# Inverse of the 64x64 triangular blocks by 64x64 tile products, two units' products issued in turn, with a new order of all work

## Chip, cores and metric

The kernel runs on one core of one Trainium2 chip. The metric is the device time of one execution in microseconds; lower is better. All times in this document are microseconds unless ns stands beside them.

## What is computed

A delta-rule attention over 4 x 8 heads of 768 tokens with 48 channels, and behind it an MLP with tanh-GELU on the heads put side by side (3,072 tokens, 384 to 2,048 to 384). The reference, cut to its core:

```
k_n = k / (np.linalg.norm(k, axis=-1, keepdims=True) + 1e-06)
state = 0
for t in range(S):
    y[:, :, t] = np.einsum('bhd,bhde->bhe', q[:, :, t], state)
    v_old = np.einsum('bhde,bhd->bhe', state, kt)
    state = state + bt * np.einsum('bhd,bhe->bhde', kt, vt - v_old)
h = x @ w_in            # x: y of all heads side by side
g = 0.5 * h * (1.0 + np.tanh(c * (h + 0.044715 * h * h * h)))
out = g @ w_out
```

## The kernel before

The sequence is cut into 12 chunks of 64 tokens. A chunk `c` holds all 32 heads, in two units `u = 2c` and `2c + 1` of 16 heads, and a unit keeps its heads as 8 pairs: one head of a pair on partitions 0 to 63, the other on 64 to 127. Inside a chunk the recurrence becomes a triangular system of 64 x 64 per head, whose inverse is found by five steps of Newton's iteration, X <- X (2 - L X). So there are three kinds of work:

- `load`, `norms` and `prep(u)`: DMA of q, k and v, norms of k, casts, transposes (T on PE, or `turn` as a DMA), the Gram products (GM, GQ, G2, G), their masked eviction on DVE (`ln`, `wpm`, `wpq`, `wp`), and the inverse.
- `chain(c)`: the part that goes from chunk to chunk: K and Q (old state times k and q), R, U (inverse times right side), S (new state), O (output), X or `turnx` (transpose for the MLP).
- `mlp(c)`: 16 groups `up0` to `up15` of three matmuls 128x256, four GELUs on ACT, two times four `down` groups of four matmuls 128x384, copies Z, and the DMA of the result.

Each inverse step `i` of a unit is: product A (L575: 8 matmuls), `rt` on DVE (2 minus A, L587), product B (L575: 8 matmuls), eviction of B as the next iterate. The iterate is kept block-diagonal in `bd`, [128, 8, 128]: the two heads of a pair stand on the two diagonal 64 x 64 blocks, the other two blocks are zero. So one matmul with a full 128 x 128 array serves a pair of heads, and the eviction of B writes two halves: `bde` (two copies of 64 partitions), `bdf` (one such copy and one of 128 partitions that multiplies by 0 or 1), or `xi` and `bdc` (a dense copy, and then two copies from there). The first iterate is made from `ln` by `X10` and `X11`. U uses the same block-diagonal matrix.

Which engine does which operation, and in what order, is a table written out by hand, `ORDER`: one word for each operation, with its engine and its PSUM bank. `Flow.emit` goes through it, gives each operation the semaphore waits that its inputs and its PSUM bank need, and writes each engine's list in that order. An engine runs its list strictly in order. `fill` words are dummy matmuls 128x512 without a reader.

Each `e.matmul` becomes two PE instructions, a weight load and a matmul. PE's list of the kernel before has 5,490 matmuls and 106 instructions that only wait.

Of the kernel before, what the change touches and what calls it, by code (L numbers as in the profile page):

```python
# [12 lines left out]
C = 64  # L13
# [4 lines left out]
beta01:a one pad1 k0x1.11:a k0x0.01:a bdz0:g upone1 wz:d fill23@0 fill20@1 fill46@0 fill16@1 fill63@4 fill26@1 half:d fill25@0 fill12@2  # L18
fill54@5 ident pad3:g k0x0.10 tmplz:d tmpl0 k0x1.00:a k0x1.10:a k0x1.01:a mmup:d pad0 mmlo:d mlo0 fill64@0 k0x0.00 mlo1 tmpl1 two:d triln1:d
triwpm3:d triwpm1:d ladj16:d fill37@1 identf k0x0.11 ident2 ladj32:d fill28@4 sq.0a:d fill65@3 mup0 k1.00 fill56@4 sum.0a triln0:d fill41@1  # L20
fill52@6 beta00 betaT0@3 betaN000 betaN001 betaN010 betaN011 k1.01 epsb k1.10:a fill45@2 beta11:a k1.11 fill22@1 beta10 sq.0b:g tabS pow.0a
eps.0a twob:d J1.1@3 sum.0b q0.1 mup1 nsa.0a v0.11 inv.0a ib.0a upone0 v0.10 pow.0b fill55@2 q0.0:a eps.0b nsa.0b sq.1:d fill36@0 kb.0 kc.1
bdz1:g k2.10 fill49@2 inv.0b ib.0b:g kb.1:g betaT1@0 kc.0 Tc.1@1 fill9@2 betaA111 betaA110 betaA101 sum.1 pow.1 eps.1:g nsq.1:g kTc.1 q1.1
fill60@4 Tb.0@2 kTb.0 Tc.0@4 kTc.0 Tb.1@1 inv.1 triwpm0:d betaA100 ib.1 GM.0@6 ln.0 kb.3:g v1.11:a v0.01 X11.0 wpm.0 kTb.1:a GM.1@4 ln.1
X10.0 v0.00:a qb.0:a Tq.0@1 wpm.1 kc.3 Tk.3@2 triln3 A1.0@0 X10.1:d kTq.0 GQ.0@4 k2.00:a kTk.3:a q1.0:a X11.1 C1.1 rj1.1 rt1.0 B1.0@0 k2.01
pad2 kb.2 wpq.0 bde10.0 kc.2:d GM.3@6 ln.3 B1.1@1 bde10.1:d bde11.0 A2.0@0 rt2.0 bde11.1 A2.1@1 rt2.1 Tk.2@3 triwpm2 B2.0@2 B2.1@0 qb.1:a
v1.00 Tq.1@1 v1.10 v1.01 wpm.3 bde21.0:d k2.11 sq.2 sum.2 bde20.0 A3.0@2 fill1@4 fill4@5 fill42@4 fill14@5 q2.0 bdf20.1 bdf21.1:d A3.1@0
rt3.0 B3.0@2 kTk.2:a GM.2@4 rt3.1 triln2 ln.2 w2.1 qb.2:a bdz4:g bdz3:g X10.3 kTq.1:a X11.3 w1.1 A1.3@0 pad5:g pow.2 B3.1@1 k3.10 GQ.1@6
wpm.2 rt1.3 kc.5 k4.10 q2.1 bdf30.0 bdf31.0 A4.0@2 rt4.0 vs.1 B1.3@0 R0b.0:g bdf30.1 bdf31.1 A4.1@1 bdz2:g wpq.1 v2.00 bdf10.3 qb.3:g
eps.2:g B4.0@2 bde41.0 nsq.2:g bde40.0 X11.2 rt4.1 q3.0 X10.2 A1.2@4 rt1.2 B4.1@1 bde41.1:d w1.0 bde40.1 Tq.2@3 kTq.2 B1.2@4 bde10.2  # L30
triwpm4:g A5.0@5 rt5.0 A5.1@1 rt5.1 bde11.2 bdf11.3:d k3.01 B5.0@2 bde50.0 A2.2@3 rt2.2 B5.1@4 bde50.1:d bde51.0 k3.00 bde51.1 B2.2@0
bde21.2 bde20.2 inv.2 A2.3@1 rt2.3 R0a.0:g U.0@4 Un.0:d B2.3@1 A3.2@0 rt3.2 q4.0 Tq.3@2 O.0@4 On.0:d fill6@3 bde21.3 qb.5:g B3.2@0 bde20.3
A3.3@1 rt3.3 kTq.3:a GQ.3@6 X.0@2 xT.0:d B3.3@1 triwpm5:g bdf30.2 bdf31.2 A4.2@0 rt4.2 bdf30.3 bdf31.3:d up4.0@2 up12.0@4 up13.0 k3.11 wpq.3
ib.2:g kb.5:g B4.2@0 up5.0 up6.0 up7.0 up14.0 A4.3@1 up15.0 up0.0@6 q3.1 tabG bde41.2:d bde40.2 up1.0 up2.0 A5.2@0 rt4.3 gelu1.0 pad4:g
kb.4:g kc.7 up3.0 B4.3@1 w2.0 kc.4:g sq.3:g sum.3 k4.00 k5.10 q4.1 gelu3.0 gelu0.0 qb.4:g T.4@2 kT.4:a T.5@4 rt5.2 bde41.3:d bde40.3:d kT.5
pow.3 eps.3:g up8.0@6 up9.0 v2.11 A5.3@0 rt5.3 k5.00:a G2.5@2 ln.5 bdz5:g kc.6:g X11.5 k4.01:a G2.4@4 S.0@0 Sn.0 ln.4 X11.4 X10.4 G.4@2 wp.4
up10.0 qb.9:a up11.0 gelu2.0 nsq.3:g qb.6:g qb.7:g k4.11 K.1@0 R.1 inv.3 ib.3:g kb.6:g kb.7:g v3.11 G.5@4 wp.5 B5.2@2 sq.4 down10.0@3 A1.4@1
down00.0@0 bde51.2 rt1.4 kc.8 down01.0 X10.5 sum.4 pow.4 eps.4:g B5.3@4 bdf50.3 B1.4@1 bde10.4 k5.01 bde11.4:d down11.0 A1.5@5 rt1.5
down02.0 k5.11 sq.5:g kc.10:g A2.4@1 v4.10 v4.11 rt2.4 turn.7 v2.10 bdf51.3 bde50.2 B1.5@4 bde10.5:d bde11.5 down03.0 Z0.0 B2.4@2 v3.10
bde21.4:d kc.9:g U.1@6 Un.1 A2.5@5 rt2.5 q5.0 down12.0 GQ.2@0 wpq.2 Q.1@6 bde20.4 A3.4@2 turn.6 v3.00:a rt3.4 G2.7@4 O.1 On.1 S.1@0 Sn.1  # L40
nsq.4:g down13.0 inv.4 ib.4:g X.1@2 B2.5@6 xT.1:d kb.9:g v4.01 sum.5 pow.5 eps.5:g kb.8:g Z1.0 bde20.5 B3.4@7 bdf30.4 turn.9 fill47@3 v3.01
ln.7 bdf31.4 v2.01:a up0.1@0 up1.1 up2.1 up3.1 bde21.5:d gelu0.1 q6.1 A4.4@2 rt4.4 qb.8:a up8.1@4 up9.1 k7.00 A3.5@3 rt3.5 B4.4@2 bde41.4
k7.11 G2.6@0 ln.6 G.7@6 wp.7 q7.0 up10.1 B3.5@3 bde31.5 bde30.5 X10.6 up11.1 gelu2.1 up4.1@0 up5.1 up6.1 G.6@6 bde40.4:d A4.5@3 k6.10:a
up7.1 down10.1@2 wp.6 k7.10 rt4.5 A5.4@4 rt5.4 up12.1@6 out11.0 gelu1.1 X11.6 A1.6@5 X11.7 X10.7 A1.7@3 rt1.7 rt1.6 k7.01 turn.8 B4.5@4
bdf40.5 q6.0 up13.1 B5.4@0 up14.1 xi5.4:d bdf41.5 B1.7@3 bdf10.7 bdc50.4 up15.1 B1.6@1 bdc51.4 bde10.6:d bde11.6 out00.0 vs.2 A5.5@5
down11.1 down12.1 q7.1 rt5.5 bdf11.7:d B5.5@5 nsa.5 gelu3.1 xi5.5 bdc50.5 A2.6@4 rt2.6 sq.7 Q.2@0 K.2@6 R.2 bdc51.5 A2.7@3 rt2.7 k6.00:a
B2.6@4 xi2.6:d bdc21.6 down00.1@5 U.2@6 Un.2 down01.1 B2.7@3 inv.5 sum.7 bde20.7:d fill27@4 O.2 bdc20.6 q5.1 G2.8@6 ln.8 A3.6@4 X10.8 ib.5:g
bde21.7 A3.7@3 rt3.7 On.2 X11.8 turnx.2 v4.00:a down13.1 Z1.1 rt3.6 G.8@6 wp.8 k6.01 vs.3 k6.11 B3.7@0 bde31.7 bde30.7 S.2@2 Sn.2 kb.10:g
B3.6@4 kb.11:g down02.1 bde30.6 A1.8@6 rt1.8 down03.1 bde31.6 kc.11:g qb.11:g Z0.1 out00.1 out11.1 A4.7@0 rt4.7 A4.6@2 B1.8@3 bdf10.8
bdf11.8 G.9@4 G2.9@6 ln.9 up4.2@0 up5.2 up6.2 B4.7@3 up7.2 up0.2@6 up1.2 up2.2 k8.10:a wp.9 rt4.6 up8.2@4 B4.6@2 bde41.6:d X11.9 bdf40.7  # L50
bdf41.7 gelu1.2 up9.2 up10.2 up11.2 up3.2 A2.8@3 qb.12:a up12.2@0 bde40.6:d A5.6@2 qb.10:g rt5.6 gelu2.2 gelu0.2 up13.2 A5.7@4 rt5.7 up14.2
rt2.8 B5.6@2 xi5.6 X10.9 A1.9@5 rt1.9 pow.7 sq.6:g B5.7@4 xi5.7 turn.10 sum.6 bdc50.7 up15.2 gelu3.2 down00.2@3 B2.8@2 bde21.8 bde20.8:d
k8.01 B1.9@4 bde10.9 K.3@6 R.3 G2.10@0 down10.2@5 q8.1 q8.0 turn.11 A3.8@2 rt3.8 kc.13:g eps.7:g bdc50.6 bdc51.6 down01.2 bdc51.7 U.3@6
# [12 lines left out]
bde50.10 up10.4 up11.4 turn.14 rt5.11 B5.11@2 up0.4@4 up1.4 up2.4 gelu2.4 nsq.8:g inv.8 bde51.10:d A2.13@0 up3.4 gelu0.4 xi5.11:d bdc51.11
# [730 lines left out]
```

## Time and profile before

| | us |
|---|---|
| median of 3 runs (262.59 to 270.14) | 262.89 |
| span of the profiled execution, first to last instruction | 258.8 |
| PE busy (matmuls, with their pipeline) | 242.1 |
| DVE busy | 209.5 |
| ACT busy | 185.1 |
| POOL busy | 136.2 |

The profile is one execution. Its rows give the engine, the line of the kernel, what is written from what, how many instructions of that kind, the busy time and the mean of one in ns; behind them stands the idle time just before these instructions and what ended it. "issue" means that the engine waited for nothing that the profile can name. The mean of a matmul holds its way through the array, some 190 ns for a narrow one; how fast matmuls follow each other is read from the timeline, where equal instructions that follow each other are one row with their start, length and count. In the windows view each row is a stretch: its length, PE's busy time with the number of matmuls, the granted clock, the busy share of the 16 DMA engines (it can pass 1 where packets run over the end of a window) and GB/s.

### The profile page before, as it was taken

How to read it: one execution, taken by the hardware profiler on the slowest of the kernel's cores; microseconds unless marked ns; L12 is line 12 of the kernel's file. 1: busy time of each engine (PE TensorE's matmuls, PEld its weight loads, DVE VectorE, ACT ScalarE, POOL GpSimd, SP SyncE). 2: the span in 40 equal slices, each digit the busy share in tenths (PEclk: the TensorE clock that was granted, in tenths of full speed). 3: DMA queues.
4: the chain of work that ended last, by engine and by line, in shares of the span. 5: the costliest groups of instructions: out<-in, count | busy, mean ns of one | idle time of the engine just before them, and what ended most of it. 6: DMA issues, size and time to landing. Idle time of an engine off the chain costs nothing.

```text
span 258.8 us, 12244 instructions
## 1 busy us (share of the span) xinstructions
PE 242.1 (94%) x5490; PEld 189.6 (73%) x5490; DVE 209.5 (81%) x358; ACT 185.1 (72%) x295; POOL 136.2 (53%) x198
## 2 busy tenths in 40 slices
PE   7769789998999999999999999989989999999994
PEld 2446669666867878778877787768868878877672
DVE  6898998988999798899999788997778879895000
ACT  0679899667786878687978879866948745754452
POOL 4469767997558978688158255643654204130000
PEclk9985999999999999999999999999999999999999
DMA  5999999879999877959729959536935720004122
GB/s 88 200 191 182 212 185 200 135 132 151 164 198 146 167 107 134 159 102 165 160 47 157 155 96 185 53 74 123 155 66 106 128 48 4 3 5 124 30 63 61
DMA packets 116788, 31.46 MB, mean 122 GB/s; under 512 B 110848, under 2 KB 115968, under 8 KB 116736
## 3 DMA queue, kind: packets, MB, share of 16 engines
q1 hardware_dynamic: 98096, 24.24, 57.4%
q0 software_dynamic: 2880, 3.15, 7.5%
q10 hardware_dynamic: 15760, 3.30, 7.4%
q8 instruction: 43, 0.70, 1.1%
q14 instruction: 9, 0.07, 0.1%
HBM read 20.64 MB, written 4.72 MB: 98 GB/s over the span
## 4 chain that ended last, share of the span: by engine, by line
PE 81%; DVE 8%; POOL 4%; issue 3%; ACTq 2%; ACT 1%; POOLq 0%
PE ps L724 24%; PE ps L735 24%; PE ps L575 20%; PE ps L530 4%; PE ps L647 3%; PE ps L670 2%; PE ps L695 2%; ACTq L432 2%; DVE rt L587 1%; PE ps L682 1%; DVE wp L534 1%; POOL nrm L458 1%; DVE ln L534 1%; PE ps L394 1%; POOL bd L564 1%
## 5 line engine op out<-in xcount | busy, mean ns | idle before, releaser
L332 ACT ACTIVATE bd<-ps 64x512 bf16<-64x512 f32 x127 | 72.8, 587 | 20.5 <-PE ps L575 18.7
L724 PE MATMUL ps<-xT,W 128*128 128x256 bf16 x576 | 76.3, 273 | 0.7 <-issue 0.7
L735 PE MATMUL ps<-W,gT 128*128 128x384 bf16 x384 | 73.8, 326 | 0.0
L728 ACT ACTIVATE gT<-ps 128x1024 bf16<-128x1024 f32 x48 | 48.5, 1020 | 15.1 <-PE ps L724 14.7
L724 PEld LDWEIGHTS ps<-xT,W 128*128 128x128 bf16 x576 | 50.7, 98 | 7.2 <-issue 1.0
L587 DVE TENSOR_TENSOR rt<-ps,two 128x512 bf16<-128x512 f32 x71 | 47.6, 683 | 5.4 <-PE ps L575 4.9
L735 PEld LDWEIGHTS ps<-W,gT 128*128 128x128 bf16 x384 | 33.0, 97 | 16.9 <-ACT gT L728 0.2
L564 POOL TENSOR_SCALAR_AFFINE_SELECT bd<-ln 64x512 bf16<-64x512 bf16 x44 | 29.1, 664 | 24.5 <-DVE ln L534 20.9
L332 DVE CAST bd<-ps 64x512 bf16<-64x512 f32 x51 | 34.8, 686 | 5.2 <-PE ps L575 4.2
L534 DVE CAST_PREDICATED wp<-mup,ps 128x1024 bf16<-128x1024 uint16 (+1 forms) x28 | 29.7, 1062 | 1.5 <-PE ps L530 1.4
L575 PE MATMUL ps<-rt,bd 128*128 128x64 bf16 x576 | 28.5, 195 | 2.0 <-DVE rt L587 1.5
L458 POOL TENSOR_TENSOR nrm<-nrm,half 128x16 f32<-128x16 f32 x9 | 26.2, 2908 | 7.6 <-DVE nrm L456 7.4
L617 POOL COPY bd<-xi 64x256 f32<-64x256 f32 x27 | 10.8, 404 | 34.6 <-DVE xi L332 19.5
L575 PE MATMUL ps<-wp,bd 128*128 128x64 bf16 (+1 forms) x576 | 27.1, 189 | 1.5 <-POOL bd L564 1.0
L575 PEld LDWEIGHTS ps<-rt,bd 128*128 128x128 bf16 x576 | 23.5, 99 | 6.7 <-DVE rt L587 2.4
L575 PEld LDWEIGHTS ps<-wp,bd 128*128 128x128 bf16 x576 | 23.0, 98 | 6.2 <-POOL bd L564 1.5
L587 DVE TENSOR_TENSOR rl<-ps,two 128x384 bf16<-128x384 f32 (+1 forms) x48 | 23.0, 484 | 4.8 <-PE ps L575 4.4
L575 PE MATMUL ps<-ln,bd 128*128 128x48 bf16 (+1 forms) x384 | 18.8, 190 | 2.8 <-issue 1.6
L575 PE MATMUL ps<-rl,bd 128*128 128x64 bf16 x384 | 18.8, 193 | 0.7 <-DVE rl L587 0.7
L575 PEld LDWEIGHTS ps<-ln,bd 128*128 128x128 bf16 x384 | 15.5, 98 | 5.2 <-issue 1.8
L575 PEld LDWEIGHTS ps<-rl,bd 128*128 128x128 bf16 x384 | 15.7, 98 | 3.0 <-DVE rl L587 1.1
L485 POOL TENSOR_TENSOR tok<-kraw,nrm 128x384 bf16<-128x384 f32 x19 | 15.6, 829 | 4.2 <-PE ps L682 2.7
(98 smaller groups left out, 327.3 us busy)
## 6 DMA issues: line engine op xcount, KB each, us to landing
qraw<-in_q_dram SPq DMA_DIRECT2D x21, 192.0 KB, 5.0
out_dram<-ob SPq DMA_DIRECT2D x21, 192.0 KB, 3.4
vraw<-in_v_dram SPq DMA_DIRECT2D x38, 96.0 KB, 3.3
kraw<-in_k_dram SPq DMA_DIRECT2D x34, 96.0 KB, 4.0
W<-in_moe_w_out_dram POOLq DMA_DIRECT2D x2, 768.0 KB, 8.5
W<-in_moe_w_in_dram POOLq DMA_DIRECT2D x2, 768.0 KB, 10.1
kraw<-in_k_dram ACTq DMA_DIRECT2D x10, 96.0 KB, 3.7
vraw<-in_v_dram ACTq DMA_DIRECT2D x10, 96.0 KB, 3.5
```

What stands on the lines that cost most here:

```text
L332: return e.activation(out, in_, ACT.Copy) if e is nc.scalar else e.tensor_copy(out, in_)
L458: if e is nc.scalar else e.tensor_tensor(nr[:, 1, hx], nr[:, 0, hx], half[:, hx], ALU.pow), reads=[nrn, "half"] + ["one", "roots"] * (c < ...
L485: A(("dve", "pool"), op("kb"), lambda e, P: e.tensor_tensor(kb, kr, nr[:, 5, hx].unsqueeze(2).to_broadcast(full), ALU.mult), reads=[f"kraw ...
L530: ins = e.matmul(o, kT[s][r, y, g, hf(a)], src)
L534: return e.copy_predicated(out.rearrange("p (x g) t -> p x g t", x=2), mask[:, 0:wd].bitcast(U16).unsqueeze(1).unsqueeze(1).to_broadcast([ ...
L564: A(("pool", "dve"), op(f"X1{a}"), lambda e, P, src=ln[m][hf(a), :, :], dst=bd[b_][hf(a), :, hf(a)], a=a: e.affine_select(out=dst, in_=src ...
L575: ins = e.matmul(P(name)[:, C * h + cs.start:C * h + cs.stop], bd[b_][:, h, :], rhs[:, h, cs], **kw)
L587: A(("dve",), op(f"rt{i}"), lambda e, P, i=i, cs=cs, cn=cn, r_=r_: e.tensor_tensor(r_[:, :, cs], P(ps(f"A{i}")).rearrange("p (h t) -> p h ...
L617: A(("pool", "dve"), op(f"bdc{i}{a}"), lambda e, P, src=xi[i_][hf(a), :, :], dst=bd[b_][hf(a), :, hf(a)]: e.tensor_copy(dst.bitcast(F32), ...
L724: ins = e.matmul(P(ph)[:, 256 * f:256 * f + 256].rearrange("p (x t) -> p x t", x=2), W1[:, j, 128 * (i + f):128 * (i + f) + 128], x_[:, :, ...
L728: A(("act",), f"gelu{i // 4}.{c}", lambda e, P, i=i, ph=ph: e.activation(g_[:, i:i + 4, :], P(ph).rearrange("p (f t) -> p f t", f=4), ACT. ...
L735: ins = e.matmul(P(po)[:, 0:DM], g_[:, f, 128 * b:128 * b + 128], W2[:, f, :], start=(f == 0), stop=(f == FC - 1))
```

## The change

The iterates are kept dense, in `xi` [128, 8, 64], and the block-diagonal tiles, their zero fills and all copies into them (`bde`, `bdf`, `bdc`, `X10`, `X11`) are gone. A product of one unit is now 16 matmuls on 64 x 64 corners of the array, two for each pair of heads. A uses the two corners whose rows and columns are the same half; B uses the other two, so its two results change halves. The Gram products are made so that the iterate and its partner lie on the right halves: the first iterate X1 comes out of the Gram product itself (`xl` holds X1 and L), so G2 and G have 32 matmuls instead of 16, for the first four units GL is added, and the mask of G2 covers 1,024 columns instead of 512. U becomes 32 matmuls on corners, instead of 16 on the full array.

A word of ORDER that begins with `+` joins the operation to the one before it on PE. Joined operations (one A and one B of two units, or a B and a U) wait for all inputs of both and are then issued in turn, two matmuls of the one and two of the other. 104 of the 252 products and U's are joined to another. The program now has 8,305 matmuls on PE and 95 instructions that only wait; The MLP's 960 matmuls and those of K, Q, S and O are unchanged. Where PE goes from full-array matmuls to corners or back, the list did so 100 times, and now 190 times.

ORDER is new as a whole. Evictions of B are 120 dense copies, 111 on ACT and 9 on DVE. ACT issues 64 DMAs instead of 33. Of the 31 dummy matmuls, eight now stand behind the last `down`.

The core of the diff (of ORDER one line of before and one of now are shown):

```diff
@@ ORDER
-wpm.2 rt1.3 kc.5 k4.10 q2.1 bdf30.0 bdf31.0 A4.0@2 rt4.0 vs.1 B1.3@0 R0b.0:g bdf30.1 bdf31.1 A4.1@1 bdz2:g wpq.1 v2.00 bdf10.3 qb.3:g
+up0.2@0 fill66@5 xi5.7:a G2.11@6 Z1.1:a ib.6:g U.3@2 B3.9@4 +A1.10@5 q8.0:s up1.2 up2.2 ln.11 G.11@6 Un.3:a rt1.10 S.3@2 kb.12:g wp.11 up3.2 xi3.9:a sq.8:a
...
@@ Flow.order
+            more = name[0] == "+"
+            o = self.by[name[1:] if more else name]
...
+            if more:
+                o.joined = self.queues["pe"][-1]
+                assert {o.side, o.joined.side} == {"same", "other"} and o.joined.joined is None
...
@@ Flow.emit
+                    runs = [x.fn(e, tile) for x in pair]
+                    last = [None, None]
+                    while runs[0] is not None or runs[1] is not None:
+                        for y in range(2):
+                            for _ in range(2 if runs[y] is not None else 0):
+                                ins = next(runs[y], None)
+                                if ins is None:
+                                    runs[y] = None
+                                    break
+                                last[y] = ins
...
@@ buffers
-    NR, NP, NB, NN, NI, NX, NG = 3, 6, 6, 4, 3, 3, 3
+    NR, NP, NN, NI, NX, NG = 3, 6, 5, 6, 3, 3
-        ln = sb("ln", [128, H, C], BF16, NN)
-        bd = sb("bd", [128, H, 128], BF16, NB)
+        xl = sb("xl", [128, 2, 2, 4, C], BF16, NN)
...
@@ prep, Gram products
-                A(PE, op("G2"), lambda e, P: gram(e, P, "G2", 0, 1, C), reads=[kTs[0]], alloc=(ps("G2"), 2), mode="t", mm=16)
-                A(PE, op("G"), lambda e, P: gram(e, P, "G", 1, None, 2 * C), reads=kTs, alloc=(ps("G"), 2), mode="t", mm=16)
+                A(PE, op("G2"), grams("G2", (0, 1, C, 0, 1), (0, 1, C, 4 * C, 0)), reads=[kTs[0]], alloc=(ps("G2"), 2), mode="t", mm=32)
+                A(PE, op("G"), grams("G", (1, 0, 2 * C, 0, 1), (1, 2, 2 * C, C, 0)), reads=kTs, alloc=(ps("G"), 2), mode="t", mm=32)
...
@@ prep, inverse
-                            ins = e.matmul(P(name)[:, C * h + cs.start:C * h + cs.stop], bd[b_][:, h, :], rhs[:, h, cs], **kw)
+                    for h in range(H):
+                        for a in range(2):
+                            yield e.matmul(P(ps(f"A{i}"))[hf(a), C * h + cs.start:C * h + cs.stop], it(hf(a), h), con(hf(a), h)[:, cs])
...
+                    for h in range(H):
+                        for a in range(2):
+                            yield e.matmul(P(ps(f"B{i}"))[hf(1 - a), C * h:C * h + C], it(hf(a), h), r_[hf(a), h, :])
-                        A(EV, op(f"bde{i}{a}"), lambda e, P, i=i, a=a: copy(
-                            e, bd[b_][hf(a), :, hf(a)], P(ps(f"B{i}"))[hf(a), :].rearrange("p (h t) -> p h t", h=H)),
                 A(EV, op(f"xi{i}"), lambda e, P, i=i: copy(e, xi[i_][:, :, :].rearrange("p h t -> p (h t)"), P(ps(f"B{i}"))),
```

PE around the chain's products of chunk 3, before: Q of chunk 3 reads the state `st1`, O reads `us1` and `wp0`, `wp1`, U reads the right side `rs1`; rows L575 are inverse products, L530 is a Gram product, L735 a `down`. A row ends with the shape of one result and the count.

```order
L670 MATMUL ps<-rs1,bd0 128x48 x8
L670 MATMUL ps<-rs1,bd1 128x48 x8
L575 MATMUL ps<-ln1,bd3 128x64 x8
L575 MATMUL ps<-rt0,bd2 128x64 x8
L647 MATMUL ps<-st1,kT0 64x48 x32
L695 MATMUL ps<-us1,wp0 64x48 x16
L695 MATMUL ps<-us1,wp1 64x48 x16
L530 MATMUL ps<-kT0 64x128 x16
L575 MATMUL ps<-rt1,bd3 128x64 x8
L735 MATMUL ps<-W20,gT2 128x384 x12
```

The same place now: L602 is Q, L646 is O, L633 is S, L675 an `up`, L527 a Gram product, L562 an A and L567 a B.

```order
L675 MATMUL ps<-xT2,W10 128x256 x6
L527 MATMUL ps<-kT0 64x64 x32
L633 MATMUL ps<-us1,tok0 64x48 x32
L675 MATMUL ps<-xT2,W10 128x256 x3
L602 MATMUL ps<-st1,kT0 64x48 x32
L646 MATMUL ps<-us1,wp0 64x48 x16
L646 MATMUL ps<-us1,wp1 64x48 x16
L562 MATMUL ps<-xl4,xi3 64x48 x2
L567 MATMUL ps<-rt0,xl0 64x64 x2
```

The last two rows then follow each other seven times more: A4 of unit 9 and B1 of unit 10, which before were 8 full-array matmuls each and stood apart, are 32 matmuls in turn. From U of chunk 3 to U of chunk 4 PE's list had 901 instructions, loads and waits counted, and now has 1,426.

ACT from U's eviction `us` in chunk 3, before: `bd` rows are evictions of B into one half (64 partitions, or 128 with the factor `up`), `xo` is O's eviction, `ob` the MLP's result, `tok` a cast of k.

```order
L332 ACTIVATE us<-ps 128x768
L332 ACTIVATE xo<-ps 128x2x8x48
L332 ACTIVATE bd<-ps 64x8x64
L338 ACTIVATE bd<-ps,up 128x8x64
L332 ACTIVATE ob<-ps 128x384
L332 ACTIVATE tok<-kraw 128x8x48
```

The same place now, `xi` being a whole dense iterate, `gT` a GELU and `sq` the squares of k:

```order
L339 ACTIVATE us<-ps 128x768
L339 ACTIVATE xi<-ps 128x512
L456 ACTIVATE sq<-kraw 128x768
L679 ACTIVATE gT<-ps 128x1024
L339 ACTIVATE xi<-ps 128x512
L339 ACTIVATE xo<-ps 128x2x8x48
```

One ACT instruction now evicts a B as a whole, where two instructions on ACT, or one on ACT and one on DVE, did before.

More of the change, by code (lines that the diff above doesn't have):

```diff
@@ L17 @@
 ORDER = """
[L18 to L21, printed above, removed]
@@ L38 @@
[L38 to L41, printed above, removed]
@@ L50 @@
[L50 to L53, printed above, removed]
@@ L197, in emit @@
                 o.tag = (o.on, count[o.on])
+                if o.joined is not None and o.joined.mm > o.mm:
+                    o.tag, o.joined.tag = o.joined.tag, o.tag
             else:
@@ L215, in emit @@
             for d in o.real | o.bankdeps | kin:
-                if d.on == e and d.dma is None and (e == "pe" and not o.fence or d.name in o.soft):
+                if d.on == e and d.dma is None and e == "pe" and not o.fence:
                     continue
@@ L241, in run @@
             def run(e):
-                for waits, o in plan[ename]:
+                mine = plan[ename]
+                for k, (waits, o) in enumerate(mine):
+                    if o.joined is not None:
+                        continue
+                    pair = [o]
+                    if k + 1 < len(mine) and mine[k + 1][1].joined is o:
+                        pair.append(mine[k + 1][1])
+                        for n, v in mine[k + 1][0].items():
+                            waits[n] = max(v, waits.get(n, 0))
                     for n, v in waits.items():
                         e.wait_ge(sems[n], v)
-                    ins = o.fn(e, tile)
-                    ins.then_inc(sems[o.tag[0]], 16 if o.dma is not None else 1)
+                    if len(pair) == 1:
+                        ins = o.fn(e, tile)
+                        if not hasattr(ins, "then_inc"):
+                            for ins in ins:
+                                pass
+                        ins.then_inc(sems[o.tag[0]], 16 if o.dma is not None else 1)
+                        continue
+                    runs = [x.fn(e, tile) for x in pair]
[8 more added lines that the diff above has]
+                                last[y] = ins
+                    for ins, x in zip(last, pair):
+                        ins.then_inc(sems[x.tag[0]], 1)
                 if ename == "sp":
@@ new lines, in gram, with grams, f, masked @@
+                        r, o = hf(p, D), 512 * p + off + wd * g
+                        yield P(ps(name))[hf(a ^ turn), o:o + C], kT[s][r, y, g, hf(a)], kT[s][r, z, g, hf(a ^ p) if z == 2 else hf(a)]
+            def grams(name, *parts):
+                def f(e, P):
+                    for part in parts:
+                        for out_, l, r_ in gram(P, name, *part):
+                            ins = e.matmul(out_, l, r_)
+                    return ins
+                return f
+            def masked(e, P, name, out, mask, wd, g, off=0):
+                return e.copy_predicated(out, mask[:, 0:wd].bitcast(U16).unsqueeze(1).unsqueeze(1).to_broadcast([128, 2, g, wd]),
+                                         P(ps(name)).rearrange("p (x r) -> p x r", x=2)[:, :, off:off + g * wd].rearrange("p x (g t) -> p x g t", g=g))
@@ L613, in prep @@
[L613 to L618 removed]
+                    two[:, cs].unsqueeze(1).to_broadcast([128, H, cn]), ALU.add), reads=["two"], frees=[ps(f"A{i}")], writes=[rn])
@@ L750, in bass_deltanet__then__act_gelu_tanh_kernel @@
         const()
-        for s in range(max(NP, NB, NN)):
+        for s in range(max(NP, NN)):
             preset(s)
```

333 lines of the change are left out of this document (127 added, 206 removed).

## Prediction

> **What bounds the kernel now.** I read the page's busy table first, then its queue table and the chain of waits, then the PE timeline.
>
> ```profile
> PE 242.1 (94%) x5490; PEld 189.6 (73%) x5490; DVE 209.5 (81%) x358; ACT 185.1 (72%) x295; POOL 136.2 (53%) x198
> q8 instruction: 43, 0.70, 1.1%
> PE 81%; DVE 8%; POOL 4%; issue 3%; ACTq 2%; ACT 1%; POOLq 0%
> ```
>
> PE is busy 94% of the span and is 81% of the chain that ended last. So the cost of PE's work decides, and so does what else can hold PE up. "issue" is 3% of the chain: PE waited there for nothing that the profile names. The second line may name it. The instruction queue moved 43 packets, 0.70 MB, so 16 KB each; PE has 5,490 matmuls and as many weight loads, 10,980 / 43 = 255 instructions per packet. Queue 8 therefore looks like PE's own code, 256 instructions of 64 bytes at a time. The timeline supports it:
>
> ```profile
> 60.18 0.72 PE L724 MATMUL ps<-xT,W 128*128 128x256 bf16 x5
> 61.58 0.61 PE L724 MATMUL ps<-xT,W 128*128 128x256 bf16 x4 [0.68 <-issue]
> ...
> 173.70 0.20 PE L575 MATMUL ps<-ln,bd 128*128 128x48 bf16 x1
> 174.79 0.33 PE L575 MATMUL ps<-ln,bd 128*128 128x48 bf16 x7 [0.89 <-issue]
> ```
>
> PE stops in the middle of an operation, after 1 of 8 matmuls or in the second of three groups of 3, where no semaphore can be waited for. The number of matmuls from one such stop to the next (x, in windows cut at seven of them):
>
> ```profile
> 46.38:61.57 15.19, 14.09 (x379) 1.00 0.86 126
> 61.57:77.17 15.60, 15.24 (x382) 1.00 1.18 182
> 77.17:108.20 31.03, 30.49 (x759) 1.00 0.88 137
> 108.20:148.22 40.02, 39.63 (x1016) 1.00 0.78 136
> 148.22:174.79 26.57, 25.68 (x636) 1.00 0.59 103
> 174.79:191.37 16.58, 15.90 (x381) 1.00 0.76 127
> ```
>
> 379, 382, 759, 1016, 636 and 381 are 3, 3, 6, 8, 5 and 3 times 126 to 127. With their loads and a few waits that is 256 instructions each time: all seven stops stand on the edges of code blocks. When does the block come? Queue 8 alone, in 0.2 us windows that start at 59.1 and at 63.4:
>
> ```profile
> q8 instruction: 1, 0.02, 30.0%
> q8 instruction: 1, 0.02, 44.0%
> ```
>
> The first packet starts at 59.1 to 59.3, takes 30.0% of 16 x 0.2 = 0.96 us, and ends near 60.2; PE goes on at 61.58, 1.4 us later. The next packet starts 1.8 to 2.0 us after PE has opened that block, takes 1.4, and 1.4 more makes 4.7 us. So one block is fetched while the one before it runs, and PE cannot open two blocks closer together than one fetch. The six cases where the trace shows this time, from the opening of a block to PE's going on in the next (second column us, last two DMA share and GB/s):
>
> ```profile
> 56.77:61.57 4.80, 4.13 (x152) 1.00 1.20 136
> 73.01:77.17 4.16, 3.81 (x151) 1.00 1.02 196
> 103.25:108.20 4.95, 4.59 (x130) 1.00 1.11 126
> 143.77:148.22 4.45, 4.07 (x154) 1.00 0.84 152
> 171.56:174.79 3.23, 2.34 (x145) 1.00 0.02 5
> 187.58:191.37 3.79, 3.11 (x152) 1.00 0.40 78
> ```
>
> Their mean is 25.38 / 6 = 4.23 us, and it rises with the DMA share (the x count a few instructions from before the cut). Now a block holds on average 227.3 / 43.3 = 5.2 us of PE's work (next part), so it hides most fetches; the stops above are the blocks whose work was shorter.
>
> [...]
>
> **PE's work, before and after.** Durations of one matmul in a stream:
>
> ```profile
> 105.24 0.49 PE L724 MATMUL ps<-xT,W 128*128 128x256 bf16 x3
> 105.66 0.44 PE L647 MATMUL ps<-st,kT 48*64 48x48 bf16 x32
> 106.03 0.41 PE L575 MATMUL ps<-rl,bd 128*128 128x64 bf16 x8
> 106.28 0.40 PE L575 MATMUL ps<-rt,bd 128*128 128x64 bf16 x8
> ...
> 252.78 2.60 PE L735 MATMUL ps<-W,gT 128*128 128x384 bf16 x15
> ...
> L724 PE MATMUL ps<-xT,W 128*128 128x256 bf16 x576 | 76.3, 273 | 0.7 <-issue 0.7
> L735 PE MATMUL ps<-W,gT 128*128 128x384 bf16 x384 | 73.8, 326 | 0.0
> L575 PE MATMUL ps<-rt,bd 128*128 128x64 bf16 x576 | 28.5, 195 | 2.0 <-DVE rt L587 1.5 <-issue 0.4
> L647 PE MATMUL ps<-st,kT 48*64 48x48 bf16 x704 | 9.2, 188 | 0.0
> ```
>
> An up matmul takes (0.49 - 0.273) / 2 = 0.109, a down (2.60 - 0.326) / 14 = 0.163, one of a full-array product (0.40 - 0.195) / 7 = 0.029, and a tile matmul on four corners in turn (0.44 - 0.188) / 31 = 0.008. From ups to tiles 105.24 + 3 x 0.109 = 105.57 to 105.66, and from tiles back 105.66 + 32 x 0.008 = 105.92 to 106.03: each change between the two shapes costs 0.10.
>
> - Removed: 240 products of 8 matmuls, 240 x 8 x 0.029 = 56 us, and U's 192, 5.6; the narrower ones take a little less.
> - Added: 240 products of 16 tile matmuls and U's 384. In 104 places two operations run in turn on unlike corners, where 32 matmuls take 32 x 0.008 = 0.26; the 37 products and 7 U alone use two corners, for which the trace has no row. Its bounds are 0.008 and twice that, since a corner's own rhythm is 4 x 0.008; I take twice. With the rest of U beside shorter partners, 104 x 0.26 + 37 x 16 x 0.016 + 7 x 32 x 0.016 + 1 = 41. If unlike corners did not overlap at all, the pairs would cost 27 more.
> - Grams: G2 and G go from 16 matmuls to 32 each, and GL is new, +4.
> - Changes of shape: 190 instead of 100, +90 x 0.096 = +8.6.
>
> Laid out matmul by matmul (narrow ones at 0.025, dummies at 0.163 x 512 / 384 = 0.22), PE's work goes from 227.3 to 221.0 us; eight dummies, 1.8, now stand behind the last down, so on the path it is -8.1.
>
> The pairing adds a wait: both units' operands must be there, and the MLP matmuls queued behind wait too. If one eviction (0.59, below) were always late, that is 104 x 0.59 = 61; the pauses of the forecast cover it.
>
> **What the other engines do.** Rows of the groups that go or grow:
>
> ```profile
> L332 ACT ACTIVATE bd<-ps 64x512 bf16<-64x512 f32 x127 | 72.8, 587 | 20.5 <-PE ps L575 18.7
> L332 ACT ACTIVATE xi<-ps 128x512 bf16<-128x512 f32 x11 | 6.3, 593 | 1.1 <-PE ps L575 1.0
> L332 DVE CAST bd<-ps 64x512 bf16<-64x512 f32 x51 | 34.8, 686 | 5.2 <-PE ps L575 4.2
> L564 POOL TENSOR_SCALAR_AFFINE_SELECT bd<-ln 64x512 bf16<-64x512 bf16 x44 | 29.1, 664 | 24.5 <-DVE ln L534 20.9
> 150.53 0.60 ACTq L432 DMA_DIRECT2D vraw<-in_v_dram  x1
> ```
>
> ACT loses 127 half evictions (-72.8), gains 100 dense ones (+59.3) and 31 more DMA issues at 0.60 (+18.6): 185 stays about 190 at most. DVE loses 34.8 and gains 20 masks that are twice as wide; even at a whole evicted tile each (0.69) that is 14, so it ends below 209.5 - 20. POOL loses 29.1. None comes near the sum below, so waits for them are covered as long as PE itself is late; in the forecast each product's operands have the fetch's pause to arrive in, and I cost them at nothing. If that cover is gone, PE's present waits stay: 258.8 - 227.3 = 31.5 us.
>
> **The term that decides.** The changed program gives PE 8,305 matmuls, 16,705 instructions with loads and waits, against 11,086: 65.3 blocks for 43.3, where the work is even smaller. Two places show it: between the Q of chain 3 and what follows, eight matmuls of a product have become pairs of two and two, sixteen a side, and on ACT two half evictions have become one, so ACT is not what PE will wait for. Cut after 193 instructions (the first edge that the stops point back to) and every 256, the 63 whole blocks up to the last two hold 3.0 us of work on average; 58 of the 63 hold under 4.23.
>
> ```profile
> 12.38 0.87 PE L530 MATMUL ps<-kT 48*64 48x64 bf16 x64 [0.26 <-DVE kT L332]
> 15.41 0.41 PE L575 MATMUL ps<-wp,bd 128*128 128x64 bf16 x8 [0.61 <-POOL bd L564]
> 0.00:258.80 258.80, 242.11 (x5490) 0.99 0.74 122
> ```
>
> - First edge: in the changed order it lies in the first inverse product, between the present first Gram (12.4) and first product (15.4): 14.
> - 63 blocks at max(own work, fetch). Fetch: bounds 3.2 and 4.95, the six rows. The DMA share is 0.74 over the span now; the same bytes over some 290 us make 0.66, between the rows of 0.40 (3.79) and 0.84 (4.45): 4.2. Sum of the 63: 267.
> - The last two blocks are MLP matmuls: 25.2 of work without the eight dummies.
> - Tail: the last matmul ends at 252.78 + 2.60 = 255.4, the span at 258.8: 3.4.
>
> Span 14 + 267 + 25.2 + 3.4 = 310. The median of the runs, 262.9, lies 4.1 above the profiled span, so **314 us**.
>
> The fetch at 3.65 gives 237 for the 63 blocks and 284 in all; at 4.6 it gives 291 and 338.
>
> [...]
>
> **Rivals.**
>
> 1. The fetch keeps ahead, and work decides. For it: only seven stops now, 31.5 us of all waits together. It needs a fetch under 3.0 us, below every row. Then today's waits stay and 262.9 - 8.1 = 254.8, faster by 3%. Chance 0.07.
> 2. The fetch falls to what the quietest row shows, 3.2, throughout: 63 blocks make 217, in all 264, within 2%. Against it: that row has a DMA share of 0.02. Chance 0.05.
> 3. Fetches do not bind, and unlike corners do not overlap: 27 more work, 254.8 + 27 = 282. Against it: the four-corner row of 0.008. Chance 0.03.
> 4. The forecast, with fetches of 3.5 us and above: 0.85. Inside it the clock could make things worse: PE pauses in nearly each block, and the page's row of the granted clock drops below 1 only in the head, where PE also paused.
>
> ```profile
> PEclk9985999999999999999999999999999999999999
> ```
>
> A stretch at half clock doubles 3.0 us of work to 6.0 and would add 1.8 per block; for 10 blocks that is 18, within the range.
>
> **How the numbers follow.** About 2% (5 us) is what a measurement of this kernel can tell from no change. Faster by more: most of rival 1, 0.06. Within: the rest of it and most of rival 2, 0.05. Slower: 0.89. The fetch from 3.6 to 4.65 gives 282 to 341 and holds 0.77 of the forecast's 0.85; rival 3 stands at the lower end: 282 to 341.
>
> **What would show it.** In the changed profile queue 8 has about 65 packets, PE's "issue" is the largest wait and falls every 128 matmuls in the middle of operations, PE's busy share is under 80%, and ACT and DVE are idle more, waiting for PE. 32 matmuls of a pair take 0.45 with their end. It would be wrong if PE opens blocks less than 3 us apart without a stop: then the fetch is deeper than I read it, and the time is near 255.

## The result, and the profile after

The changed kernel takes 334.78 us (median of 4 runs, 332.94 to 335.44) beside 264.16 for the kernel before (median of 4 runs): a ratio of 1.269, 95% interval 1.257 to 1.280. One run of the kernel before, 270.14, fell in a slower state of the chip; ratios and differences, here and below, leave such runs out. In a second comparison, further below, it took 328.26, a ratio of 1.251 (1.244 to 1.258). The forecast was 314, with a range of 282 to 341. The profiled execution took 335.33 with a span of 333.6. The lines of its page that answer to those shown of before: busy times, clock, DMA share, the instruction queue, the chain of waits.

```profile
PE 262.0 (79%) x8305; PEld 190.1 (57%) x8305; DVE 189.8 (57%) x301; ACT 158.9 (48%) x248; POOL 93.9 (28%) x131
PEclk9997755677589979797999979999999999999999
DMA  6999992299379680793990596451559110321024
q8 instruction: 65, 1.06, 1.4%
PE 75%; issue 19%; DVE 4%; ACT 0%; ACTq 0%
```

All four engines wait more than before. The instruction queue moves 65 packets instead of 43, and "issue", time in which PE waited for nothing that the profile names, has grown from 3% to 19% of the chain, 63 us. The list of what PE waited for (us in total, times, longest) says the same:

```profile
PE ps L567 <- issue: 25.0, 15, 4.2
PE ps L527 <- issue: 10.9, 10, 2.1
PE ps L562 <- issue: 7.9, 7, 2.5
PE ps L602 <- issue: 6.6, 4, 2.7
PE ps L407 <- DMA braw<-in_beta_dram: 5.3, 1, 5.3
...
PE ps L675 <- DVE rt L569: 1.6, 1, 1.6
```

The wait for a DMA in the fifth row is in the head. The largest wait for a result of another engine is 1.6 us, once. Where PE stops is read from its timeline, here in the middle of a B and an A that are issued in turn:

```profile
140.85 0.19 PE L567 MATMUL ps<-rt,xl 64*64 64x64 bf16 x1
142.18 0.21 PE L567 MATMUL ps<-rt,xl 64*64 64x64 bf16 x1 [1.14 <-issue]
...
142.27 0.21 PE L567 MATMUL ps<-rt,xi 64*64 64x64 bf16 x2
...
142.52 0.21 PE L562 MATMUL ps<-wp,xi 64*64 64x32 bf16 x2
```

PE stands still between the first and the second matmul of a couple, where no semaphore stands. The next pair then runs whole, from 142.27 to 142.73, 0.46 us for 32 matmuls. Five stretches from one block edge to the next, in windows (length, PE's busy time and matmuls, further engines, clock, DMA share, GB/s):

```profile
126.59:130.32 3.73, 3.09 (x126) 1.95 (x127) 2.31 (x4) 1.96 (x4) 0.22 (x1) 1.00 0.16 31
130.32:133.87 3.55, 2.35 (x128) 1.95 (x127) 3.04 (x3) 2.03 (x3) 0.00 (x0) 1.00 0.02 5
138.08:142.17 4.09, 2.96 (x130) 2.38 (x129) 2.23 (x4) 2.52 (x4) 2.45 (x1) 0.93 1.03 131
142.17:146.28 4.11, 2.85 (x126) 2.33 (x127) 3.07 (x5) 2.30 (x4) 0.00 (x0) 1.00 1.07 157
146.28:151.39 5.11, 3.00 (x128) 2.11 (x127) 2.35 (x4) 2.82 (x5) 1.47 (x1) 1.00 1.33 195
```

126 to 130 matmuls each time: with their loads and a few waits one block of 256 instructions. Counted through the whole trace, from the start of one matmul to the start of the next less what the first takes in a stream, PE stops for more than 0.15 us on 48 of the 65 edges of blocks (193 instructions and every 256 from there), 71 us in sum; by the same count the kernel before did so on 7 of 43, 5 us. That is 66 us more, where the span grew by 75. (The list of waits counts from the modelled end of a matmul and has 62 us at these edges.) And the stages, cut at the block edges:

```profile
16.04:95.14 79.10, 52.94 (x1788) 40.26 (x1787) 42.88 (x64) 36.64 (x58) 34.35 (x44) 0.70 0.90 117
95.14:200.12 104.98, 80.91 (x3059) 58.31 (x3057) 68.57 (x102) 50.25 (x80) 35.52 (x35) 0.93 0.75 109
200.12:304.56 104.44, 91.59 (x3187) 67.67 (x3184) 64.59 (x94) 54.56 (x80) 13.07 (x16) 1.00 0.38 69
304.56:333.60 29.04, 27.20 (x195) 18.76 (x192) 2.30 (x4) 9.22 (x11) 0.00 (x0) 1.00 0.24 56
```

The first three are 14, 24 and 25 blocks: 5.65, 4.37 and 4.18 us each. The DMA share falls along with them, 0.90, 0.75 and 0.38.

### The profile page after: what moved, and what is told of

The parts are those of the page before. It is cut to its first block, busy times and chain, and to the rows that moved or that the text cites. A ratio compares the mean times of both kernels' runs of the same rounds, so it can differ in the third digit from the quotient of the medians.

```text
span 333.6 us, 17631 instructions
## 1 busy us (share of the span) xinstructions
PE 262.0 (79%) x8305; PEld 190.1 (57%) x8305; DVE 189.8 (57%) x301; ACT 158.9 (48%) x248; POOL 93.9 (28%) x131
## 3 DMA queue, kind: packets, MB, share of 16 engines
q0 software_dynamic: 2880, 3.15, 6.0%
## 4 chain that ended last, share of the span: by engine, by line
PE 75%; issue 19%; DVE 4%; ACT 0%; ACTq 0%
PE ps L675 22%; PE ps L686 21%; PE ps L567 8%; PE ps L562 7%; PE ps L527 6%; PE ps L602 2%; PE ps L396 2%; PE ps L625 2%; PE ps L495 1%; PE ps L646 1%; PE ps L633 1%; DVE xl L532 1%; DVE rt L569 1%; DVE nrm L458 1%; PE ps L658 1%
## 5 line engine op out<-in xcount | busy, mean ns | idle before, releaser
L339 ACT ACTIVATE xi<-ps 128x512 bf16<-128x512 f32 x111 | 63.9, 596 | 89.3 <-PE ps L567 63.1
L675 PE MATMUL ps<-xT,W 128*128 128x256 bf16 x576 | 79.3, 287 | 2.4 <-DVE rt L569 1.6
L675 PEld LDWEIGHTS ps<-xT,W 128*128 128x128 bf16 x576 | 54.3, 102 | 13.9 <-DVE rt L569 1.9
L527 PE MATMUL ps<-kT 48*64 48x64 bf16 x1536 | 26.9, 208 | 10.9 <-issue 10.9
L567 PE MATMUL ps<-rt,xi 64*64 64x64 bf16 x768 | 24.6, 205 | 12.3 <-issue 12.2
L532 DVE CAST_PREDICATED xl<-mlo,ps 128x1024 bf16<-128x1024 uint16 (+1 forms) x28 | 29.5, 1064 | 7.4 <-PE ps L527 7.1
L527 PEld LDWEIGHTS ps<-kT 48*64 48x64 bf16 x1536 | 20.9, 119 | 16.5 <-issue 15.2
L567 PE MATMUL ps<-rl,xi 64*64 64x64 bf16 x768 | 23.1, 204 | 6.6 <-issue 6.5
L567 PEld LDWEIGHTS ps<-rt,xi 64*64 64x64 bf16 x768 | 18.8, 116 | 15.5 <-issue 14.3
L562 PE MATMUL ps<-xl,xi 64*64 64x48 bf16 (+1 forms) x768 | 23.1, 198 | 4.7 <-issue 4.7
L567 PEld LDWEIGHTS ps<-rl,xi 64*64 64x64 bf16 x768 | 18.0, 117 | 12.3 <-issue 11.6
L562 PE MATMUL ps<-wp,xi 64*64 64x64 bf16 (+1 forms) x768 | 22.4, 197 | 3.2 <-issue 3.2
L562 PEld LDWEIGHTS ps<-wp,xi 64*64 64x64 bf16 x768 | 18.0, 118 | 9.4 <-issue 7.1
L562 PEld LDWEIGHTS ps<-xl,xi 64*64 64x64 bf16 x768 | 17.8, 115 | 4.2 <-issue 2.5
```

Of the source, the lines that this page charges most:

```text
L339: return e.activation(out, in_, ACT.Copy) if e is nc.scalar else e.tensor_copy(out, in_)
L527: ins = e.matmul(out_, l, r_)
L532: return e.copy_predicated(out, mask[:, 0:wd].bitcast(U16).unsqueeze(1).unsqueeze(1).to_broadcast([128, 2, g, wd]), P(ps(name)).rearrange( ...
L562: yield e.matmul(P(ps(f"A{i}"))[hf(a), C * h + cs.start:C * h + cs.stop], it(hf(a), h), con(hf(a), h)[:, cs])
L567: yield e.matmul(P(ps(f"B{i}"))[hf(1 - a), C * h:C * h + C], it(hf(a), h), r_[hf(a), h, :])
L675: ins = e.matmul(P(ph)[:, 256 * f:256 * f + 256].rearrange("p (x t) -> p x t", x=2), W1[:, j, 128 * (i + f):128 * (i + f) + 128], x_[:, :, ...
```

## The experiments

Theory (code): PE's instructions come in blocks of 256, one block is fetched while the one before it runs, and the changed list gives PE too little work per block to hide the fetch. Rivals: PE's own work (corners that don't overlap, changes of shape), waits of joined operations for both units' operands, late evictions or loads.

**Joined operations apart** (the changed kernel; same matmuls, so the rival of corners or of common waits would show).

```diff
-            if more:
-                o.joined = self.queues["pe"][-1]
-                assert {o.side, o.joined.side} == {"same", "other"} and o.joined.joined is None
```

> The changed kernel, with joined operations issued one behind the other instead of in turn; same matmuls, 26 waits fewer. Code theory (a block of 256 PE instructions cannot be opened sooner than about 4.5 us after the one before it, which is what 288.5 us for the 63 middle blocks give): the same count of blocks, 65.2 for 65.3, so 334.8 plus about 2, 330 to 342. Rival, corners: what the pairs overlap is lost, 104 x 0.26 = 27 us more work, if PE's work decides: 355 to 362. Rival, pair waits: the time is lost because both units' operands must be there together; without the joining it would fall toward 263.

Measured: 327.74, ratio 1.251 (1.216 to 1.287). It is 2% under the changed kernel's 334.78 and a little under the code theory's range, so it ran again beside the changed kernel on one chip, with a third kernel that waits for both operands and then issues the two operations whole:

```diff
-                if o.joined is not None and o.joined.mm > o.mm:
-                    o.tag, o.joined.tag = o.joined.tag, o.tag
...
-                            for _ in range(2 if runs[y] is not None else 0):
+                            for _ in range(32 if runs[y] is not None else 0):
```

> The changed kernel once more, beside the next two on one chip: 333 to 336.

> The joined operations issued apart once more, beside the changed kernel on one chip. If the 7 us were the joining: 2% under the changed kernel again. If they were chance of that chip or run: equal within 0.5%.

> The changed kernel, in which two joined operations still wait for the inputs of both together, but the first is then issued whole and the second behind it. Same instructions. If the common wait costs the 2%: like the changed kernel, 333 to 336. If the issue in turn costs them: like the kernel with operations apart, 326 to 329.

Measured: in turn 328.26, ratio 1.251 (1.244 to 1.258); apart 329.26, 1.256 (1.251 to 1.262); common wait without mixing 327.25, 1.247 (1.239 to 1.255). The three can't be told apart; the 7 us lay between two comparisons, not in the joining, and the changed kernel too is 7 us lower in this one. So the expected 333 to 336 missed; why the two comparisons differ is not known, but 5 of the 7 us lie in the stops, 66 us in sum here and 71 in the first trace. Pairing neither helps nor harms the time here: the rivals of corners and of common waits both fall as its cause. Issue in turn does save work on PE: late in the trace (behind 200 us, clock 1.00) the 32 matmuls of a pair start within 0.25 us in turn (median of 16 pairs) and within 0.40 apart (8 pairs), and PE is busy for 257.9 us in turn, 267.7 apart and 269.5 with the common wait alone. The stops take it back: 66, 57 and 54 us.

**Less code** (the changed kernel; B is left out for one half of the heads).

```diff
                     for h in range(H):
-                        for a in range(2):
+                        for a in range(1):
                             yield e.matmul(P(ps(f"B{i}"))[hf(1 - a), C * h:C * h + C], it(hf(a), h), r_[hf(a), h, :])
...
```

> The changed kernel, with each second product (B) left out for one half of the heads: 8 matmuls instead of 16, 960 matmuls and 1,920 instructions less, all evictions and waits as before. Code theory: 57.8 blocks instead of 65.3, with 4.5 us as the least time of a block the sum of the blocks falls by 33 us, so about 300, 295 to 306. Rival, PE's work: 960 x 0.008 to 0.016 us less, 320 to 327. Rival, waits for evictions and data: nothing changes there, 330 or more.

Measured: 306.51, ratio 1.170 (1.137 to 1.204), 28 and 22 us less than the changed kernel's two results. That is more than the work rival allows (8 to 15) and less than the code theory's 33, just outside its range of 295 to 306; 27 of its 57 edges still stop, for 41 us in sum, where the changed kernel's two traces have 71 and 66.

**More code** (the kernel before; S three times, the Gram products of width 64 twice).

```diff
-                        ins = e.matmul(o, kT[s][r, y, g, hf(a)], src)
+                        for _ in range(2 if wd == C else 1):
+                            ins = e.matmul(o, kT[s][r, y, g, hf(a)], src)
...
-                        ins = e.matmul(at("S", P, hf(p), a, x, g), tok[ss[x]][hf(a), 1, 2 * g + p, :], ub[hf(a), x, p, g, :])
+                        for _ in range(3):
+                            ins = e.matmul(at("S", P, hf(p), a, x, g), tok[ss[x]][hf(a), 1, 2 * g + p, :], ub[hf(a), x, p, g, :])
```

> The kernel before, with each matmul of S issued three times and each of the Gram products that are 64 wide twice, into the same places: 1,216 matmuls, 2,432 instructions more. Code theory: 52.8 blocks instead of 43.3; with 4.2 to 4.5 us as the least time of a block the sum of the blocks grows by 40 to 44 us, of which some falls into waits that are there anyway: 290 to 308. Rival, PE's work: 1,216 x 0.009 = 11 us, 270 to 275.

Measured: 292.33 (one run) beside 260.24 and 263.59, 29 to 32 us more, in the code theory's range and outside the rival's. Its stops are 24 us on 20 of 53 edges, where the kernel before has 5 us on 7 of 43. At the head of what PE waited for stand now:

```profile
PE ps L684 <- issue: 11.2, 7, 3.3
PE ps L531 <- issue: 6.2, 8, 1.8
```

L684 and L531 are the lines of S and of the Gram products: the new stops stand where the code was added.

**Waits as code** (the kernel before, with instructions that touch no array).

```diff
+                    if ename == "pe":
+                        for _ in range(7):
+                            e.wait_ge(sems["pe"], 1)
```

> The kernel before, with seven waits behind each of PE's operations for a value that was reached at the start; they add 2,335 instructions to PE's list (two waits go into one instruction) and no matmul. Code theory: an instruction is code whatever it does; 52.4 blocks instead of 43.3, the sum of the blocks with 4.2 to 4.5 us as the least time grows by 21 to 27 us, 276 to 292 in all, with stops on the edges of 256 instructions counted with these waits. Rival: it is matmuls or their weight loads that take the time, not code; then only the waits' own time is added, and no stop moves: 262 to 270.

```profile
q8 instruction: 52, 0.85, 1.1%
```

Measured: 325.90 (one run) beside 262.86, above both. 52 packets for 52.4 blocks: the waits fill blocks too. But the waits cost time of their own, (324.2 - 258.8) / 2,335 = 28 ns each if all of it is theirs, which lengthens the blocks to 5.9 us, so that only some 8 us of stops are left. The run tells nothing about the time of a fetch.

**Narrower MLP matmuls** (both kernels; the same instructions with half the columns, the other half left out).

```diff
-                            ins = e.matmul(P(ph)[:, 256 * f:256 * f + 256].rearrange("p (x t) -> p x t", x=2), W1[:, j, 128 * (i + f):128 * (i + f) + 128],
-                                           x_[:, :, j, :], start=(j == 0), stop=(j == J - 1))
+                            ins = e.matmul(P(ph)[:, 256 * f:256 * f + 256].rearrange("p (x t) -> p x t", x=2)[:, :, 0:64], W1[:, j, 128 * (i + f):128 * (i + f) + 128],
+                                           x_[:, :, j, 0:64], start=(j == 0), stop=(j == J - 1))
...
-                            ins = e.matmul(P(po)[:, 0:DM], g_[:, f, 128 * b:128 * b + 128], W2[:, f, :], start=(f == 0), stop=(f == FC - 1))
+                            ins = e.matmul(P(po)[:, 0:DM // 2], g_[:, f, 128 * b:128 * b + 128], W2[:, f, 0:DM // 2], start=(f == 0), stop=(f == FC - 1))
```

> The changed kernel with the same halved MLP matmuls, PE's own work again 62 us less. Code theory: nearly nothing of it shows, since blocks stand at the fetch's time already; with 4.5 us as the least time the sum of the blocks falls by 14: 318 to 326. Rival, PE's work or waits for data: 62 less, 270 to 280.

> The kernel before, with every matmul of the MLP over half of its columns (up 128 instead of 256, down 192 instead of 384; the other halves are left out). Same instructions; PE's own work falls by 576 x 0.055 + 384 x 0.081 = 62 us. Code theory: the blocks' mean work falls to 3.6 us, under the fetch, so most blocks stop: the sum of the blocks with a least time of 4.2 to 4.5 us falls by 36 to 42 only, 221 to 232 with PE's other waits. Rival, PE's work decides: near 263 - 62 = 201, or DVE's 209 busy us as the next bound: 201 to 215.

Measured: the changed kernel 317.19, 11 to 18 us less for 62 us of work taken away (reckoned from rows at full clock; PE's busy time fell from 262.0 to 224.4), just under the code theory's 318 and far above the rival's 280, with stops on 50 of 65 edges; its mean clock was 0.80. So neither PE's work nor its clock sets the time where a block waits for its code. The kernel before took 254.39, ratio 0.972 (0.964 to 0.980): 7 us less, where the code theory expected 31 to 42 and the rival 48 to 62, so both missed. The chain of waits of this narrower kernel before shows what holds it:

```profile
DVE 37%; PE 26%; DMA 10%; ACT 9%; POOL 8%; issue 7%; SPq 2%; ACTq 1%; POOLq 0%
```

PE had 81% of that chain; now DVE has the largest share, and "issue" 7%. With less work on PE the kernel before meets a second bound some 7 us below, a chain in which DVE leads, and the expectation did not count it.

**Fewer bytes beside the code** (q, k and v of chunks 3 to 11 cut to an eighth of the heads, in both kernels; the rest is left out).

```diff
-                        A(("sp", "act"), f"{n}{c}.{a}", lambda e, P, a=a, view=view: e.dma_start(raw["q"][s][hf(a), :, :], view[a, c]),
+                        A(("sp", "act"), f"{n}{c}.{a}", lambda e, P, a=a, view=view: e.dma_start(raw["q"][s][hf(a), 0:2 * H if c < 3 else 2, :], view[a, c][:, 0:2 * H if c < 3 else 2, :]),
...
-                    xs = slice(0, H) if x is None else slice(4 * x, 4 * x + 4)
+                    xs = slice(0, H if c < 3 else 1) if x is None else slice(4 * x, 4 * x + 4)
```

> The changed kernel, with the loads of q, k and v of chunks 3 to 11 cut to an eighth of the heads (as many DMAs, an eighth of the bytes). Code theory with transfers in the way of the code packets: the time from opening a block to going on falls from about 4.5 us toward the 3.2 to 3.8 of the quietest rows, 285 to 300 in all. Code theory where that time is the queue's own: unchanged, 330 to 336. Rival, late loads: waits for q, k, v go away, but stops stay at each block edge as long as they are.

> The kernel before with the same cut of the loads of q, k and v of chunks 3 to 11 to an eighth of the heads (control for the changed kernel with few loads, which lost 17 to 24 us by it). Code theory: the loads cost the changed kernel time by way of the code packets alone; here only 7 us of stops can shrink, and other waits take part of that: 257 to 264. Rival, late loads or busy queues cost as such: 10 us or more less here too, 240 to 253.

```profile
16.21:83.06 66.85, 47.55 (x1789) 36.88 (x1788) 41.84 (x63) 36.08 (x58) 33.58 (x43) 0.77 0.65 92
```

Measured: the changed kernel 310.75, ratio 1.187 (1.153 to 1.220), 18 to 24 us less and between its two expectations; the kernel before 259.49, ratio 0.988 (0.985 to 0.992), 3 us less, as its stops are (from 5 to 2 us). The window holds the same 14 blocks of the head as the first stage above: 66.9 us instead of 79.1, at a DMA share of 0.65 instead of 0.90 (and a clock of 0.77 instead of 0.70). So 0.87 us of each of the 14 blocks (12.2 / 14) went with the bytes beside the code, though PE's list is the same, and the loads cost the changed kernel time by way of its code; that a fetch waits among the other transfers is the author's reading of it. The gain is less than the 35 to 50 us that fetches of 3.2 to 3.8 us would give: stops remain on 43 of 65 edges, for 53 us.

**A kernel before with its stops filled** (11 MLP operations moved forward into the six blocks that end in a stop; one of the six moves in ORDER as an example).

```diff
-v10.00:a B3.19@4
+v10.00:a down01.7 down02.7 B3.19@4
...
-A4.18@5 down01.7 down02.7 down12.7
+A4.18@5 down12.7
```

> The kernel before with 11 operations of the MLP (6 ups and 5 downs) moved forward by a few places, each pair into the block of 256 PE instructions that ends in a stop (the stops after 45.9, 76.6, 107.6, 147.7, 173.7 and 190.5 us), so that these blocks hold 0.65 to 1.3 us more work. Code theory: the stops there (0.50 + 0.54 + 0.55 + 0.57 + 1.07 + 0.88 = 4.1 us) shrink by 3 to 4 us in sum: ratio 0.984 to 0.992 to the kernel before. Rival, the stops hide behind other waits or the moved work delays the chain as much: ratio 0.996 to 1.01.

Measured: ratio 1.007 (1.003 to 1.011), so slower by a little, not faster, in the rival's range. From the block edge near 94 us on, its stops fell from 3.0 to 0.5 us in sum, as meant; ahead of that, the one in the ups of chunk 1 grew, from 0.68 in the row that the prediction shows to 1.7. That row of what PE waited for, and a row for DVE:

```profile
PE ps L575 <- DVE rt L587: 2.1, 6, 0.7
...
PE ps L724 <- issue: 1.7, 1, 1.7
```

And its chain; in that of before, DVE had 8% and issue 3%:

```profile
PE 82%; DVE 12%; ACT 2%; issue 2%; DVEq 0%; ACTq 0%
```

Part of the stops came back as one, and by the count above they fell only from 4.9 to 3.7 us in all, while DVE's share of the chain rose by 4 points. So this run does not tell what the stops of the kernel before are worth, and why it is 0.7% slower stays open; with fewer bytes, where they fell by 3 us, the time fell by 3. No version here that does all of the work beats the kernel before.

## Why the prediction was right

- **The deciding term.** Blocks of 256 instructions, one fetch each, stops on their edges: 65 packets were forecast and came, "issue" is the largest wait, PE's busy share is 79% (under 80% was forecast), and adding code to the kernel before or taking it from the changed one moved the time as blocks do and not as work does. The stops on block edges grew by 66 us, the span by 75. What these runs don't show by themselves is why the next block is not asked for earlier; that only one is fetched ahead is read from the stops and the packets: in the changed kernel, the next packet starts 1.1 to 4.9 us after PE has gone on behind a stop.
- **Sizes.** The sum was 14 + 267 + 25.2 + 3.4 = 310 for the span, and the trace has 16.0 + 288.5 + 29.0 = 333.6. The last two terms, 28.6, measured 29.0. The mis-sized term is that of the 63 blocks, 21.5 us short: they took 288.5 / 63 = 4.58 on average. By the prediction's own sums (291 for a fetch of 4.6) that is a fetch near 4.6; the range ended at 4.65, so the time fell into it with little to spare. Nearly all of the 21.5 stands in the first stage: 14 blocks at 5.65 instead of 4.2, 14 x 1.45 = 20. The forecast took one fetch time from the mean DMA share over the span, 0.66; but the transfers stand in the head, at 0.90. And the trace of before had longer fetches there. The prediction names seven stops and measures six; the first one, at 46.38 us, ends a block that PE opened at 39.46:

```profile
39.46:46.38 6.92, 6.40 (x129) 1.00 1.28 199
```

  With 6.92 the mean of the seven is (25.38 + 6.92) / 7 = 4.61, and 4.6 gives the prediction's 338 in all, nearer to the 334.78 than its 314. A fetch that PE doesn't wait for can be timed too: behind the openings at 19.81, 26.87 and 34.44 the packets start at 24.00, 30.43 and 36.62, take 0.88, 0.88 and 1.43, and with 1.4 from there to going on that makes 6.5, 5.8 and 5.0 us, an estimate. PE's long blocks in the head of the kernel before (7.1, 7.6 and 5.0 us from these openings to the next) hid them; the changed kernel's short ones (52.94 / 14 = 3.8 us of busy PE each in the first stage) do not. 12 of its 14 blocks there end in a stop. How far that goes is seen in two blocks of the changed kernel, as windows from opening to going on:

```profile
32.90:40.24 7.34, 3.76 (x127) 3.07 (x126) 3.77 (x6) 2.54 (x3) 1.83 (x1) 0.73 1.25 194
156.41:159.66 3.25, 2.17 (x150) 1.58 (x142) 2.05 (x3) 2.77 (x5) 1.23 (x2) 1.00 0.02 5
```

  The first one's code packet lies between 37.6 and 38.8 us. The transfers there, by queue (packets, MB, share of the 16 engines):

```profile
q0 software_dynamic: 99, 0.19, 83.9%
q1 hardware_dynamic: 195, 0.04, 21.8%
q8 instruction: 1, 0.02, 4.6%
```

  That block took 7.34 us at a DMA share of 1.25, with the queue that brings the MLP's weights (q0; its 3.15 MB in all are their four transfers of 768 KB) busy beside it, and the other 3.25 at 0.02. The forecast's quietest row, 3.23, was near the least that the trace shows (one block, from 264.30 to 266.79, took 2.49 with a stop at its end; PE had not stopped at its opening, and the packet started only 0.2 us behind it); its upper one, 4.95, was no ceiling.
- **The first rival, a fetch that keeps ahead.** The prediction gave it 0.07. The runs decide for the stops: 48 stops with a mean of 71 / 48 = 1.5 us in the changed kernel, so here the crossing from block to block is hidden only while a block's work is longer than the fetch.
- **PE's work and the pairs.** A pair took 0.46 us, with its end, for 0.45 forecast, and two products that run alone behind 200 us start their 16 matmuls within 0.23, 0.015 each for 0.016. Issued apart, a pair takes 0.15 us longer, 104 x 0.15 = 16 us as an estimate, where the rival put 27; that cost no time that shows (329.26 apart, 328.26 in turn), since the stops were shorter by 9 us (57 for 66). Whether the work fell by the 8 us that the sum gives is not shown by any run.
- **Other engines.** DVE, 189.8, is near the estimate of 189.5. POOL, 93.9, is 13 under its 107: 27 copies `bd<-xi`, 10.8 us, went as well. ACT is 158.9, 26 under the 185 of before, where "about 190 at most" was said: the 31 DMA issues, 18.6, were counted in, which the page doesn't count as busy, and 19 evictions with the factor `up`, 12.8, were forgotten among what goes. None bounds, as forecast.
- **The clock.** The granted clock fell to 0.91 in the mean, and to 0.70 in the first stage. The forecast left room for that (18 us for ten blocks). In a block without a stop it costs: eight downs take 2.74 us from 89.04, at a granted clock of 0.50, (2.74 - 0.336) / 7 = 0.34 each for 0.163 before, and the block that opens at 88.69 takes 6.5 us though no stop ends it. But the stage's blocks are mostly held by their fetch, and the narrower MLP ran at a clock of 0.80 without being slower.

```profile
89.04 2.74 PE L686 MATMUL ps<-W,gT 128*128 128x384 bf16 x8
```

- **What would have been left without the fetch** isn't settled: no run takes the fetch away.

## What to carry to other kernels

Count PE's instructions, not only its cycles: here 256 of them, weight loads and waits included, had to hold more work than a fetch takes (3.2 to 3.7 us at a DMA share of 0.02 to 0.16, 4.1 to 5.1 at 1.03 to 1.33, 7.3 at 1.25 beside the MLP's weights), and a rewrite that splits its matmuls, as this one goes from 5,490 to 8,305, can lose that. Look for stops inside an operation, "issue" in the list of waits, and count the matmuls between them; if they are multiples of one number, as here of 126 to 130, suspect the code. And time the fetch from every packet of the instruction queue, stage by stage, also where PE does not wait for it: in the head of the kernel before it took 5 to 7 us behind long blocks, and the rewrite's short blocks brought that to light.

## What was not expected of the hardware

- A code fetch varies more than twofold with the transfers beside it, from 3.25 us at a DMA share of 0.02 to 7.34 at 1.25 from opening a block to going on, although the packet itself takes only 0.9 to 1.5 us; cutting the bytes of the loads shortened the changed kernel by 18 to 24 us without touching PE's list.
- Seven waits behind each operation for a value long reached, which fill 2,335 instructions, made the span 65 us longer, up to 28 ns an instruction.
- The changed kernel gave 334.78 in one comparison and 328.26 in another, 2% apart, where the kernel before gave 262.59 to 265.43 and 260.80 to 262.92. The cause is not known; such a kernel is best compared within one session.
